# Moving accumulations between VectorE and ScalarE, filling PSUM banks earlier, and loading the first left-over tiles from SBUF

## The chip, the cores and the metric

The kernel runs on one core of a Trainium2 chip. The metric is the device time of one execution in microseconds (us). A core has a matrix engine (TensorE, PE in the profile), a vector engine (VectorE, DVE), an engine for activation functions that also copies and casts (ScalarE, ACT), a general one (GpSimd, POOL), and SyncE (SP), which here only issues DMAs. Each engine works through its own queue of instructions in order and waits on semaphores for what other engines have to finish first. PE reads from the on-chip memory SBUF and writes to PSUM, from which VectorE and ScalarE take the results. DMAs are issued from SP's queue and from ScalarE's queue (SPq and ACTq in the profile), and an issue stands in its engine's queue like any other instruction.

## The reference

One transformer block over a sequence of 2048 tokens with 576 features, in fp32. From a condition vector come six modulation vectors; then an attention with a memory carried over four segments of 512 tokens, and a gated MLP with 4608 hidden features:

```python
h = _layernorm(x) * (1 + ca) + sa
x = x + ga * _A_ref(h, A_wq, A_wk, A_wv, A_wo, A_beta)
h = _layernorm(x) * (1 + cb) + sb
g = _silu(h @ w_gate)
u = h @ w_up
x = x + gb * ((g * u) @ w_down)
```

The change touches the MLP and the passage from the attention to it, nothing inside the attention.

## The kernel before

**Precision.** Every fp32 operand of a matmul is split in two: a rounded part (`...h`, a cast on ScalarE) and the rest (`...l`, a subtraction on VectorE). A product takes three matmuls: high by high, high by low, low by high. So each operand costs one ScalarE and one VectorE instruction before PE can use it.

**Seven products for eight.** The MLP works on two halves of the tokens (t = 0 and 1, 1024 each) and, in each, on 18 blocks p of 256 hidden features. Inside a block the matrices are cut 2 by 2 and multiplied in seven products with sums and differences of the quarters (Winograd's form of Strassen's method). The operands for the tokens, seven sums m = 1 to 7 of them, lie in the tile `y`. The weights' sums are built by `sum_o` (L1410) in the tile `O`, and `prep_w` (L1413) splits them into `wh` and `wl`.

**A round.** One block p takes 14 steps k (loop at L1797): seven for the gate (z = 0) and seven for the up projection (z = 1). `step` (L1486) issues seven matmuls through `prod` (L1446): three for each of two pieces of 128 features, and one for the left-over 32 features, which are stored three times over (rows 0 to 31, 32 to 63 and 64 to 95: high, low, high) in the tiles `R[0]` and `R[1]` (`wr` in the profile). Results gather in the PSUM banks A, B and C, from which ScalarE copies (`copy_t`, L1480, and L1499) and VectorE adds (`fin`, L1462). The result of a round is the hidden block `AC`.

**Down projection.** The hidden block of round p is multiplied by `w_down` during round p + 1, between its steps. In `plain` rounds (t = 0, p = 0 to 6, and the last two blocks of both halves) eight groups of 12 matmuls do it. In the other rounds (t = 0, p = 7 to 15; t = 1, p = 0 to 15) it is done with seven products too: 14 groups c = 0 to 13 of six matmuls each (`down`, L1565), spread over the steps by `CH` (L37): one group a step, two in steps 4 and 11, none in steps 6 and 13. Group c belongs to product `POS[c // 2]`. Each product has an accumulator `acc` in SBUF that runs over all rounds.

**Banks and accumulators.** The results of a group go to a PSUM tile `pd` of tag `dn`, of which there are two, so group c + 2 uses that of group c. Most groups start a new sum in the bank, and VectorE adds it to the accumulator afterwards (L1584). The groups listed in `PA7` (L54), for t = 0, do otherwise: ScalarE first copies the accumulator into the bank (L1563), the matmuls add onto it, and ScalarE copies it back (L1580). The tile is claimed, and the accumulator put into it, at the top of the step in which the group runs (L1808 to L1810, `down_new`). In p = 7 the products 1, 5, 6 and 7 start anew, without an accumulator.

**Order.** The order of all this is written out by hand in the loop: what is issued in a step is in the order of the lines L1799 to L1917, for each engine. Subtractions on VectorE that belong to casts (`later`) run at the top of the next step, before the next products.

**Preparing the second half's operands.** While rounds p = 1 to 6 of t = 0 run, a generator `prep2` (L1264) builds the token operands of t = 1: twice per step, in steps 1 to 13, one turn is taken from it (L1915 to L1917). First five rows of 128 tokens are normalised: statistics on VectorE, two small instructions on GpSimd, the scaling on ScalarE (L1307), a store to DRAM (L1308), and the load of the row after next (L1289). Then for each of six pieces the columns are loaded back, transposed by PE into a `dn` bank (L1337), scaled, and the seven operands are formed, split and stored (`opr`, L1269).

**The first left-over tiles.** Before the first round, during the last projection of the attention (a loop over n = 0 to 31, L1721), the sums of the first left-over rows are built in a tile `RB` and split into `RH` (high, on ScalarE) and `RB` (low, on VectorE). `store_rb` (L1401) writes them three times to DRAM (`rD`) from ScalarE's queue at n = 12. `prep_r` (L1381) reads them back into `R[0]` and `R[1]` with six loads in SP's queue at n = 17 and 18. Later rounds read their left-over tiles from the same place in DRAM. At n = 24 ScalarE's queue issues the store of some weight sums (`store_o`). The loads of the first token operands `y` stand in SP's queue ahead of `prep_r`, and the stores of the projection's rows (`xD`, L883) among and behind it.

Of the kernel before, what the change touches and what calls it, by code (L numbers as in the profile page):

```python
# [15 lines left out]
P = 128  # L16
# [6 lines left out]
L = 512  # L23
# [29 lines left out]
P7 = 7  # L53
PA7 = (1, 3, 7, 9, 13)  # L54
WC = 4
# [46 lines left out]
def f32(ap):  # L102
    return ap.bitcast(F32)
# [3 lines left out]
def block(ctx: ExitStack, tc: tile.TileContext, x, wqk, wv, wo, beta, wgu, wrm, wd, c, w_mod, wm01, out):  # L107
# [1156 lines left out]
    def prep2(x2p):  # L1264
# [29 lines left out]
        for j, (sn, i) in enumerate(rows):  # L1294
# [10 lines left out]
            nc.gpsimd.tensor_scalar(nb, mv[:, 0:1], rs[:, 0:1], -1.0, op0=ALU.mult, op1=ALU.mult)  # L1305
            yield
            nc.scalar.activation(xl, xl, AF.Identity, scale=rs[:, 0:1], bias=nb[:, 0:1])  # L1307
            nc.sync.dma_start(xhD[sn][:, i, :], xl)  # L1308
            yield
            if j < 3:  # L1310
                load_row(j + 2)
            for _ in range(3):
                yield
        xbs = (xb, xl2[:, :L].rearrange("p (a b) -> p a b", b=P))
# [16 lines left out]
        for kb in range(3):  # L1331
            n = P if kb < 2 else 96
            for hv in range(2):
                for kh in range(2):
# [8 lines left out]
                    if j < 12:  # L1343
                        load(j)
                h00, h10, h01, h11 = [ha[:n, k, 256 * b:256 * b + 256] for k in range(2) for b in range(2)]
                nc.gpsimd.tensor_tensor(t3[:n], h11, h10, op=ALU.subtract)
                yield from opr(kb, hv, 0, h00)
                nc.gpsimd.tensor_tensor(h10, h10, h00, op=ALU.subtract)
                yield from opr(kb, hv, 5, t3[:n])
                yield from opr(kb, hv, 2, h11)  # L1350
                yield from opr(kb, hv, 3, h10)
                nc.gpsimd.tensor_tensor(h11, h11, h10, op=ALU.subtract)
                yield from opr(kb, hv, 1, h01)
                yield from opr(kb, hv, 4, h11)
                nc.gpsimd.tensor_tensor(h01, h01, h11, op=ALU.subtract)
                yield
                yield from opr(kb, hv, 6, h01)
# [37 lines left out]
    def split_rb(j):  # L1395
        r = RB[j]
        rh = RB[j, 1] = opl.tile([P, 7, P], F32R, tag="RH", name="RH")
        nc.scalar.copy(rh, r)
        later.append(lambda: nc.vector.tensor_tensor(r.bitcast(F32R), r, f32(rh), op=ALU.subtract))

    def store_rb(j):  # L1401
# [158 lines left out]
    def down_new(t, p, c):  # L1560
        pd = PD[c] = ps.tile([P, 2, L], F32, tag="dn", name="pd", bufs=2)
        if t == 0 and c in PA7 and (p > P7 or POS[c // 2] in (2, 3, 4)):
            nc.scalar.copy(pd[:, :, :288], down_acc(t, c))  # L1563

    def down(t, p, c):  # L1565
        m, q = POS[c // 2], c % 2
        ah, al = AP[p % 2, m]
        dh, dl = DP[p % 2, m]
        pd = PD.pop(c)
        new = p == (0 if t else P7) and m not in (2, 3, 4)  # L1570
# [8 lines left out]
        if on_act:  # L1579
            nc.scalar.copy(o, pd[:, :, :288])  # L1580
        elif new:
            nc.vector.tensor_copy(o, pd[:, :, :288])
        else:
            nc.vector.tensor_tensor(o, o, pd[:, :, :288], op=ALU.add)  # L1584

    def plain(t, p, c):
# [54 lines left out]
    with tc.manual_schedule():  # L1641
# [79 lines left out]
        for i in range(4):  # L1721
            for h in range(2):
                for c in range(WC):
# [16 lines left out]
                    elif n == 10:  # L1740
                        split_rb(0)
                    elif n == 12:
                        store_rb(0)
                    elif n in (17, 18):
                        prep_r(0, 0, n - 17)
                    if n == 24:
# [31 lines left out]
        for t in range(2):  # L1778
            for p in range(NPR):
# [17 lines left out]
                for k in range(14):  # L1797
# [8 lines left out]
                    while acts:  # L1806
                        acts.pop(0)()
                    if prev is not None and not is_plain(*prev):  # L1808
                        for j in range(CH[k]):
                            down_new(*prev, chunk + j)  # L1810
                    if dl and k in HP:
# [176 lines left out]
```

## Time and profile before

| | |
|---|---|
| median of three runs | 1814.87 us (1814.16 to 1815.64) |
| the profiled execution | 1814.78 us |
| its span, from the first to the last instruction | 1813.1 us |
| PE busy | 1765.0 us, 97% of the span |
| VectorE busy | 1495.2 us, 82% |
| ScalarE busy | 994.7 us, 55% |
| GpSimd busy | 485.3 us, 27% |

From 832 to 1152 us the rounds run whose down projections use `PA7`, nine in all; there PE is busy for 306.52 of 320 us, VectorE for 291.09, ScalarE for 199.08 and GpSimd for 135.13. The MLP begins near 543 us.

How to read the rows: times are in us, those of one instruction in groups in ns. A row of instructions in order of time has its start, its duration, engine, line, operation and tiles (output <- input), and in square brackets the idle time of the engine before it and what ended that (its releaser). A row of waits has the waiting instruction, what it waited for, the sum in us, how many times, and the longest. A group's row has the count, the busy time and the mean in ns, and behind the second bar the idle time just before. A window's row has its bounds and length, the busy time of PE, PE's weight loads, VectorE, ScalarE and GpSimd with the number of instructions, then the granted clock of PE, the DMA engines' busy share and GB/s. PE's matmuls overlap: a matmul on 512 columns is listed with 390 ns and the next starts 227 ns after it.

### The profile page before, as it was taken

To read this page: it belongs to the slowest core of one execution; us is meant where nothing else is said; L and a number is where in the kernel's file an instruction comes from. 1 tells how busy PE (TensorE), PEld (TensorE's weight loads), DVE (VectorE), ACT (ScalarE), POOL (GpSimd) and SP (SyncE) were. 2 spreads that over 40 slices of the span, in tenths; PEclk is the share of its full clock that TensorE was granted. 3 is DMA by queue.
4 is the path that set the end of the run, shared out by engine and by line. 5 is a ranking of instruction groups with operands and counts; after the bars stand their busy time and mean duration, and the time that the engine had idled before them with its cause. 6 is when DMAs were issued, how large, how long until landed. Compare 5 with 4: busy or idle time off the path is not lost.

```text
span 1813.1 us, 31431 instructions
## 1 busy us (share of the span) xinstructions
PE 1765.0 (97%) x10945; PEld 1494.4 (82%) x10945; DVE 1495.2 (82%) x3326; ACT 994.7 (55%) x2151; POOL 485.3 (27%) x748
## 2 busy tenths in 40 slices
PE   8999999999997999999999999999999999999999
PEld 5888867767776888888887888888888888888888
DVE  7567489999975787878999998868888888888886
ACT  6344578778864454544665666534544544544542
POOL 2100146555670654453354443100000000000000
PEclk9999999999998999999999999999999999999999
DMA  8678765577668677654443444495334324324331
GB/s 296 225 241 279 234 206 172 170 194 216 185 234 281 207 241 223 209 157 126 174 136 129 156 161 148 139 314 150 100 103 124 105 87 130 107 80 130 107 103 53
DMA packets 149190, 309.85 MB, mean 171 GB/s; under 512 B 28184, under 2 KB 60376, under 8 KB 147240
## 3 DMA queue, kind: packets, MB, share of 16 engines
q1 hardware_dynamic: 134824, 253.98, 45.8%
q10 hardware_dynamic: 14208, 53.86, 7.6%
q8 instruction: 87, 1.43, 0.3%
q14 instruction: 71, 0.58, 0.1%
HBM read 193.73 MB, written 113.33 MB: 169 GB/s over the span
## 4 chain that ended last, share of the span: by engine, by line
PE 73%; DVE 6%; DMA 3%; ACT 2%; issue 1%; POOL 1%; ACTq 0%; SPq 0%; DVEq 0%; POOLq 0%
PE A L1453 22%; PE pd L1576 14%; PE C L1453 11%; PE pd L1598 7%; PE B L1453 6%; PE av L768 3%; PE pw L876 2%; PE s L713 2%; PE s L742 2%; DVE wl L1418 1%; DVE sg L1529 1%; PE pn L1012 1%; DMA rD<-RB 1%; DVE acc L1584 1%; DMA wr<-rD 1%
## 5 line engine op out<-in xcount | busy, mean ns | idle before, releaser
L1453 PE MATMUL A<-y,wh 128*128 128x512 f32 x1152 | 404.2, 391 | 2.2 <-ACT B L1499 1.5
L1584 DVE TENSOR_TENSOR acc<-acc,pd 128x576 f32<-128x576 f32 x292 | 218.3, 750 | 66.2 <-PE pd L1576 59.6
L1418 DVE TENSOR_TENSOR wl<-O,wh 128x256 fp32r<-128x256 f32 x504 | 245.5, 492 | 11.3 <-ACT wh L1417 10.8
L1453 PEld LDWEIGHTS A<-y,wh 128*128 128x128 f32 x1152 | 216.5, 188 | 42.5 <-ACT tb L1482 1.9
L213 DVE CUSTOM_DVE_ANT_0 junk<-s,tri 128x384 bf16<-128x384 f32 (+3 forms) x512 | 218.4, 486 | 22.7 <-PE s L742 8.7
L1453 PE MATMUL A<-y,wl 128*128 128x512 f32 x576 | 224.7, 390 | 0.0
L1576 PE MATMUL pd<-dh,ah 128*128 128x288 f32 x700 | 209.4, 299 | 13.5 <-ACT pd L1563 8.6
L1576 PE MATMUL pd<-dl,ah 128*128 128x288 f32 x700 | 206.1, 294 | 0.0
L1576 PE MATMUL pd<-dh,al 128*128 128x288 f32 x700 | 205.1, 293 | 0.0
L1453 PE MATMUL C<-y,wh 128*128 128x512 f32 x576 | 202.5, 392 | 0.0
L1417 ACT CAST wh<-O 128x256 fp32r<-128x256 f32 x504 | 199.4, 405 | 4.8 <-issue 2.9
L1523 DVE TENSOR_TENSOR al<-sg,ah 128x512 fp32r<-128x512 f32 x219 | 160.7, 734 | 10.9 <-ACT ah L1522 10.7
L1522 ACT CAST ah<-sg 128x512 fp32r<-128x512 f32 x219 | 136.0, 621 | 54.0 <-DVE sg L1477 38.9
L1576 PEld LDWEIGHTS pd<-dh,ah 128*128 128x128 f32 x700 | 131.4, 188 | 31.6 <-ACT pd L1563 12.0
L1408 POOL TENSOR_TENSOR O<-O 128x256 f32<-128x256 f32 x132 | 114.1, 882 | 137.6 <-DMA O<-in_wgu_dram 66.2
L749 ACT ACTIVATE Pt<-s 128x512 f32<-128x512 f32 x256 | 135.4, 598 | 22.3 <-PE s L742 13.2
L1576 PEld LDWEIGHTS pd<-dl,ah 128*128 128x128 f32 x700 | 132.4, 189 | 12.3
L1576 PEld LDWEIGHTS pd<-dh,al 128*128 128x128 f32 x700 | 132.1, 189 | 0.0
L1453 PE MATMUL A<-y,wr 128*128 128x512 f32 x288 | 113.9, 395 | 10.4 <-DMA wr<-rD 10.4
L1453 PEld LDWEIGHTS C<-y,wh 128*128 128x128 f32 x576 | 108.0, 188 | 18.9
L1453 PEld LDWEIGHTS A<-y,wl 128*128 128x128 f32 x576 | 108.3, 188 | 15.4
L1469 ACT ACTIVATE sg<-sg 128x512 f32<-128x512 f32 x73 | 46.2, 633 | 124.5 <-DVE sg L1468 124.5
(422 smaller groups left out, 4320.0 us busy)
## 6 DMA issues: line engine op xcount, KB each, us to landing
wr<-rD SPq DMA_DIRECT2D x213, 112.0 KB
O<-in_wgu_dram SPq DMA_DIRECT2D x36, 512.0 KB
O<-oD SPq DMA_DIRECT2D x36, 512.0 KB
oD<-O ACTq DMA_DIRECT2D x34, 512.0 KB
ks<-kD SPq DMA_DIRECT2D x64, 216.0 KB
qs<-qD SPq DMA_DIRECT2D x64, 216.0 KB
O<-in_wgu_dram SPq DMA_DIRECT2D x36, 384.0 KB
y<-yD SPq DMA_DIRECT2D x11, 1024.0 KB
```

Of the source, the lines that this page charges most:

```text
L213: nc.vector.tensor_tensor_reduce(junk[:, :n], bank[:, o:o + n], tri[:, L - n:], 1.0, -3e38, op0=ALU.add, op1=ALU.max, accum_out=mcol[u][0] ...
L749: nc.scalar.activation(pt[:, h], bank, AF.Exp, scale=SCALE)
L768: nc.tensor.matmul(av[u][32 * h:32 * h + 32, 128 * j:L], lhsT=vq[s][:, j, VW * hh:VW * hh + 32], rhs=pt[:, h, c:c + L - 128 * j], start=(j ...
L1408: eng.tensor_tensor(o[:, d], o[:, a], o[:, b], op=op)
L1417: nc.scalar.copy(wh, o)
L1418: later.append(lambda: nc.vector.tensor_tensor(wl, o, f32(wh), op=ALU.subtract))
L1453: nc.tensor.matmul(bank, lhsT=a, rhs=b, start=(first and n == 0), stop=(n == 6), skip_group_check=not first)
L1522: nc.scalar.copy(ah, src)
L1523: later.append(lambda: nc.vector.tensor_tensor(al, src, f32(ah), op=ALU.subtract))
L1576: nc.tensor.matmul(pd[:, i, :288], lhsT=a[:, tk], rhs=w, start=(first and k == 0), stop=(k == 2), skip_group_check=not first)
L1584: nc.vector.tensor_tensor(o, o, pd[:, :, :288], op=ALU.add)
L1598: nc.tensor.matmul(pd[:, i, :288], lhsT=a[:, tk], rhs=w, start=(k == 0), stop=(k == 5))
```

## The change

There are three parts. (1) `PA7` names nine groups in place of five, and groups 7, 9 and 13 leave it. A `pd` tile is no longer claimed at the top of the step: `down` claims those of its own and the next group if that has not been done (t = 1: its own alone), and at its end, for t = 0, that of group c + 2, or of the first groups of the next round; ScalarE's copy of the accumulator into the bank is issued there, right behind the emptying of the same bank. (2) In `prep2` a row's scaling stands four turns behind its statistics, with its store and the load of the row after next directly behind it; one turn is added between the two transposes of a piece and one is taken out before the last operand; the subtractions stand earlier, and the operands come in the order 0, 2, 1, 5, 3, 4, 6. The number of turns stays the same. (3) `first_r` at n = 12 copies the first left-over tiles with six DMAs in ScalarE's queue from `RH` and `RB` straight into `R[0]` and `R[1]`; the loads at n = 17 and 18 are gone, and the store to DRAM stands at n = 28.

```diff
-PA7 = (1, 3, 7, 9, 13)
+PA7 = (0, 1, 2, 3, 4, 6, 8, 10, 12)
...
-            yield
+            for _ in range(4):
+                yield
             nc.scalar.activation(xl, xl, AF.Identity, scale=rs[:, 0:1], bias=nb[:, 0:1])
             nc.sync.dma_start(xhD[sn][:, i, :], xl)
-            yield
             if j < 3:
                 load_row(j + 2)
-            for _ in range(3):
-                yield
+            yield
...
+                    if kh == 0:
+                        yield
                 h00, h10, h01, h11 = [ha[:n, k, 256 * b:256 * b + 256] for k in range(2) for b in range(2)]
                 nc.gpsimd.tensor_tensor(t3[:n], h11, h10, op=ALU.subtract)
+                nc.gpsimd.tensor_tensor(h10, h10, h00, op=ALU.subtract)
                 yield from opr(kb, hv, 0, h00)
-                nc.gpsimd.tensor_tensor(h10, h10, h00, op=ALU.subtract)
-                yield from opr(kb, hv, 5, t3[:n])
                 yield from opr(kb, hv, 2, h11)
-                yield from opr(kb, hv, 3, h10)
                 nc.gpsimd.tensor_tensor(h11, h11, h10, op=ALU.subtract)
                 yield from opr(kb, hv, 1, h01)
+                nc.gpsimd.tensor_tensor(h01, h01, h11, op=ALU.subtract)
+                yield from opr(kb, hv, 5, t3[:n])
+                yield from opr(kb, hv, 3, h10)
                 yield from opr(kb, hv, 4, h11)
-                nc.gpsimd.tensor_tensor(h01, h01, h11, op=ALU.subtract)
-                yield
                 yield from opr(kb, hv, 6, h01)
...
+    def first_r():
+        for z in range(2):
+            for c in range(3):
+                v = RB[0] if c == 1 else f32(RB[0, 1])
+                nc.scalar.dma_start(f32(R[z][32 * c:32 * c + 32]), v[32 * z:32 * z + 32])
...
     def down_new(t, p, c):
-        pd = PD[c] = ps.tile([P, 2, L], F32, tag="dn", name="pd", bufs=2)
+        pd = PD[t, p, c] = ps.tile([P, 2, L], F32, tag="dn", name="pd", bufs=2)
         if t == 0 and c in PA7 and (p > P7 or POS[c // 2] in (2, 3, 4)):
             nc.scalar.copy(pd[:, :, :288], down_acc(t, c))
 
+    def ahead(t, p, c):
+        v = (p + c // 14, c % 14)
+        if (t, *v) not in PD and not is_plain(t, v[0]):
+            down_new(t, *v)
+
     def down(t, p, c):
+        for j in range(c, c + 2 - t):
+            ahead(t, p, j)
...
-        pd = PD.pop(c)
+        pd = PD[t, p, c]
...
+        if t == 0:
+            ahead(t, p, c + 2)
...
                     elif n == 12:
+                        first_r()
+                    elif n == 28:
                         store_rb(0)
-                    elif n in (17, 18):
-                        prep_r(0, 0, n - 17)
...
-                    if prev is not None and not is_plain(*prev):
-                        for j in range(CH[k]):
-                            down_new(*prev, chunk + j)
```

## The prediction

> **What bounds the kernel now.** I read the page's head first, then the list of what TensorE (PE) waited for, because PE is busy almost throughout.
>
> ```profile
> span 1813.1 us, 31431 instructions
> PE 1765.0 (97%) x10945; PEld 1494.4 (82%) x10945; DVE 1495.2 (82%) x3326; ACT 994.7 (55%) x2151; POOL 485.3 (27%) x748
> ...
> PE A L1453 <- DMA wr<-rD: 10.4, 1, 10.4
> PE pd L1576 <- ACT pd L1563: 8.6, 8, 1.8
> ...
> PE pd L1576 <- DVE acc L1584: 4.9, 7, 1.1
> ...
> PE A L1453 <- ACT B L1499: 1.5, 1, 1.5
> ...
> PE pt L1337 <- DVE acc L1608: 0.8, 2, 0.4
> PE A L1453 <- ACT tb L1482: 0.7, 1, 0.7
> ```
>
> PE has 48 us of idle time in the span (1813.1 - 1765.0), and no edit here takes a matmul away, so those 48 us and slowed matmuls are all there is to win. The waits quoted add up to 26.9 us, and each of the three edits points at some of them: the second and third line at the accumulators, the first at the left-over tiles, the last three at the operand preparation. Next, two windows: one in the first half of the MLP, while sums are accumulated in seven products, and one in the second half.
>
> ```profile
> 900.00:1000.00 100.00, 95.73 (x510) 82.20 (x509) 93.51 (x141) 62.88 (x137) 42.02 (x42) 1.00 0.44 145
> ...
> 1300.00:1400.00 100.00, 100.00 (x545) 88.09 (x544) 86.77 (x163) 48.66 (x113) 0.00 (x0) 1.00 0.34 105
> ```
>
> The columns are PE, PEld, DVE, ACT and POOL busy time. In the first half VectorE (DVE) is at 94% and PE has gaps; in the second DVE is at 87%, GpSimd (POOL) is idle, and PE has none. The same matmuls run in both, so the second half gives the floor. I take it from the chain of waits, from the second step of a round (bank C) to that of a later round.
>
> ```profile
> 889.79 1.62 PE C L1453 x7
> ...
> 1137.91 1.62 PE C L1453 x7
> ...
> 1160.27 1.60 PE pd L1598 x12
> ...
> 1224.91 1.59 PE C L1453 x7
> ...
> 1292.03 1.59 PE C L1453 x7
> ```
>
> The first two rows are seven rounds apart: 248.12 / 7 = **35.45 us** a round. The last two are two rounds apart: 67.12 / 2 = **33.56 us**. (The row between is a group of another stage, for edit 3.) Nine rounds (t = 0, sums of p = 7 to 15) thus lose up to 9 x 1.89 = 17.0 us, of which the waits show 13.5 and slower starts after them the rest.
>
> **Edit 1: accumulators.** One round in order of time shows both waits.
>
> ```profile
> 881.86 1.41 DVE L1584 TENSOR_TENSOR acc<-acc,pd 128x576 f32<-128x576 f32 x2
> ...
> 881.97 0.62 ACT L1522 CAST ah<-sg 128x512 fp32r<-128x512 f32 x1 [1.56 <-DVE sg L1529]
> ...
> 882.66 0.40 PE L1576 MATMUL pd<-dh,ah 128*128 128x288 f32 x1 [0.83 <-DVE acc L1584]
> ...
> 885.84 0.63 ACT L1469 ACTIVATE sg<-sg 128x512 f32<-128x512 f32 x1 [2.94 <-DVE sg L1468]
> ...
> 888.05 0.64 ACT L1563 COPY pd<-acc 128x576 f32<-128x576 f32 x1
> ...
> 888.74 0.40 PE L1576 MATMUL pd<-dh,ah 128*128 128x288 f32 x1 [1.82 <-ACT pd L1563]
> ```
>
> At 882.66 group 6 waits for its bank: DVE, late in its queue, empties groups 4 and 5 only then. At 888.74 group 7 waits for ScalarE (ACT) to put its accumulator into the bank; that copy stands in ACT's queue behind a Silu that waited 2.94 us for DVE, and behind DMA issues and casts. After the change groups 0 to 4, 6, 8, 10 and 12 are ACT's, so 0, 2, 4, 6, 8, 10 and 12 leave DVE, and 7, 9 and 13 come to it; group 7 needs no copy at all, and group 6 gets its copy behind the emptying of group 4, in the same bank. So the 1.8 us wait loses its cause, and the 0.8 us one comes to hang on ACT in place of DVE. The prices:
>
> ```profile
> L1418 DVE TENSOR_TENSOR wl<-O,wh 128x256 fp32r<-128x256 f32 x118 | 68.6, 592 | 0.0
> ...
> L1584 DVE TENSOR_TENSOR acc<-acc,pd 128x576 f32<-128x576 f32 x72 | 53.2, 748 | 9.8 <-PE pd L1576 8.5
> ...
> L1580 ACT COPY acc<-pd 128x576 f32<-128x576 f32 x42 | 26.9, 642 | 28.5 <-PE pd L1576 28.5
> ...
> L1563 ACT COPY pd<-acc 128x576 f32<-128x576 f32 x40 | 25.7, 642 | 0.0
> ```
>
> (groups by line of 845 to 1145 us). DVE loses 4 x 0.748 = 3.0 us a round: from 0.9351 x 35.45 = 33.1 to 30.1. ACT gains 4 emptyings and 4 fillings, 8 x 0.642 = 5.1 us: from 0.6288 x 35.45 = 22.3 to 27.4, which is 81% of a round of 33.8. Both fit under PE. What is late next: in every second round ACT casts a left-over tile in the step of groups 4 and 5, just ahead of emptying group 4, so group 6 may still wait a few tenths there; and group 1's new filling sits behind DVE's emptying of group 13, with ACT's casts of the next operands queued behind it, which are used a round later. I leave 0.3 us a round for all this, an estimate a little under half of the 0.83 us wait: 9 x (35.45 - 33.86) = **14.3 us** gained. Bounds: 17.0 above; below, what rivals A (6.3) and C (0) give.
>
> Against this stands a rule of the Trainium skill ("SBUF — State Buffer", section "Who interferes with whom"): a VectorE instruction with two SBUF inputs contends with a GpSimd instruction that reads SBUF, and one with at most one SBUF input, as the accumulation from PSUM is, does not. The trace agrees as far as it goes: wl, with two SBUF inputs, takes 592 ns here and 492 over the whole run (row under rival A). By that rule the change takes away the very instructions that never met GpSimd; the sum by it is rival A's.
>
> In the second half the bank is now claimed just ahead of its use and not one step ahead; claiming issues nothing, and PE has no gap to lose or win there: 0, covered by the full PE of the 1300 window.
>
> **Edit 2: first left-over tiles.** Today they go SBUF to DRAM and back:
>
> ```profile
> 535.06 0.81 ACTq L1404 DMA_DIRECT2D rD<-RH  x2
> ...
> 536.18 14.41 DMA rD<-RB
> 550.66 0.32 SPq L1384
> ...
> 551.49 3.73 DMA wr<-rD
> ...
> 555.36 0.77 PE L1453 MATMUL A<-y,wr 128*128 128x512 f32 x1 [10.45 <-DMA wr<-rD]
> ...
> 559.34 0.53 PE L1453 MATMUL A<-y,wl 128*128 128x512 f32 x1
> ```
>
> The store takes 14.41 us, the load 3.73, and PE stands for 10.45. Then it runs slowly: nine matmuls in 555.36 to 559.34, 0.44 us apart, against 1.59 / 7 = 0.227 in the chain rows: 3.98 - 2.04 = 1.9 us more. Ceiling 12.4 us. After the change six 112 KB copies go from SBUF straight into the tiles, half the bytes of the store. Bounds on their landing: 3.73 us after 535.06, or 14.41 us after 536.18, when 550.6 would leave 5.7 us of the wait. Half the bytes of the slow row, 7.2 us, puts them at 543.4, ahead of PE's need (555.36 - 10.45 = 544.9). I take this: no wait for them.
>
> What stands behind the new issues:
>
> ```profile
> SPq L1361 <- DMA rD<-RH: 7.7, 1, 7.7
> ...
> L1384 ACTq DMA_DIRECT2D wr<-rD x3: 328/378/432, 1193.8 to 1194.7; - x3
> ...
> 536.86 0.58 ACT L855 CAST hh<-pto 128x512 fp32r<-128x512 f32 x1
> ...
> 539.61 0.37 PE L876 MATMUL pw<-woh,hh 128*128 128x288 f32 x1 [0.58 <-DVE xr L881]
> ...
> 547.22 0.32 SPq L1361 DMA_DIRECT2D y<-yD  x1
> ...
> ACT cu L1482 <- PE A L1453: 10.1, 1, 10.1
> ```
>
> Three more issues on ACT's queue are 3 x 0.378 = 1.1 us; the cast hh behind them ends at 537.44, PE needs it at 539.61, so 2.2 us cover that. But the first row shows that an issue can wait for an earlier DMA that it has nothing to do with (a load on SP's queue, 7.7 us for a store from ACT's). If ACT's last copies wait so for the first to land, at some 541, hh ends near 542 and PE is 2.5 us late. I take 1.5 of these. The six loads leave SP's queue, so the y load at 547.22 and what follows it come no later. The store to DRAM now stands, with three issues, ahead of the copy cu, for which PE's third step waits; today ACT idles 10.1 us there. For this I take 0.5. Together 12.4 - 2.0 = **10.4 us**; bounds 12.4 and, with rival B, 4.
>
> **Edit 3: operand preparation.** The same instructions in other places: a row's scaling stands four turns behind its statistics and not one, the next row's load directly behind a store, and subtractions earlier.
>
> ```profile
> ACT ha L1307 <- POOL nb L1305: 8.0, 3, 4.2
> ACT xl L1307 <- POOL nb L1305: 7.5, 2, 3.9
> ```
>
> Up to 4.2 us ACT stands before a scaling, and what is queued behind it, the copies B and tb, is what PE waits for in the 1.5 and 0.7 us rows. Three turns more are one and a half steps, each of 7 matmuls for products and, mostly, 12 for sums, 3.2 us (1.6 each in the chain rows): 4.8 us, more than the 4.2. With the 0.8 us of transposes that wait for DVE the ceiling is 3.0 us; new is that the first load of the next part follows the last row's store by one turn and not four, and holds SP's queue until that store has landed. I put that at 1 us, an estimate from the two 0.4 us waits that PE has at these transposes today: 3.0 - 1.0 = **2.0 us**, bounds -1.0 (the new wait alone) and 3.0.
>
> **The sum** is made against the profiled execution's 1814.78 us, of which 1.7 lie around the span, unchanged, and which stands 0.09 us under the median of 1814.87: 1814.78 - 14.3 - 10.4 - 2.0 = **1788.1 us**.
>
> **Rivals.**
>
> A: DVE stays the bound of the nine rounds. For it: 94% busy, and its instructions are longer where POOL works beside it.
>
> ```profile
> L1418 DVE TENSOR_TENSOR wl<-O,wh 128x256 fp32r<-128x256 f32 x504 | 245.5, 492 | 11.3 <-ACT wh L1417 10.8
> ```
>
> If the denser rest collides so much more that half of the 3.0 us is eaten, DVE has 31.6 us of work a round. On a line between the two windows (86.8%: nothing lost; 93.5%: 1.89 us lost) this settles at a round of about 34.75 (90.9%, 1.2 lost): 9 x 0.7 = 6.3 us gained, **1796.1 us**. Against it: the freed instructions lie in the steps where PE waits, since groups 0, 2, 4 and 6 leave DVE there, and 7, 9 and 13 come back only later in the round.
>
> B: the left-over tiles land as late as the store does, 14.41 us after their issue. Of the 12.4 us the wait's rest of 5.7 and the slow restart of 1.9 stay, with the 0.5 of above: 4.3 gained, **1794.2 us**. For it: the loads that filled the DMA engines then are still there. Against it: half the bytes, and no second trip.
>
> C: the wait only changes its name. The bank of group c + 2 is that of group c, so a filling can't start before the bank is emptied; if ACT empties group 4 as late as DVE did, group 6 waits for ACT, and the nine rounds gain nothing: **1802.4 us**. Against it: in the round shown ACT idles for the 1.56 us up to 881.97, just where emptying and filling (1.28 us) would go.
>
> D, on the other side: ACT becomes the bound of the nine rounds. Its emptyings wait for PE, 28.5 us in 42, 0.68 each (the L1580 row), in order, with everything behind them. Four more cost 2.7 us a round, and the copies 5.1: 7.8. Today 35.45 - 22.3 = 13.2 us of ACT's round are idle; if they can't take this in, because each of them waits for a fixed point of PE or DVE, the round grows to 43.2 and the kernel by 9 x 7.8 = 70 less 12.4: **1872 us**. It decides from where more than 9.4 us of idle time stay in a round: 27.4 + 9.4 = 36.8, that is 12.4 / 9 above today's 35.45. Against it: in the second half such waits shrink as PE runs on without gaps.
>
> **How the numbers follow.** The forecast has 0.57, A 0.17, B 0.12, C 0.06, D 0.05; 0.03 are for several small losses that cancel the gain. The predicted time is the forecast's, 1788. All ceilings together, 17.0 + 12.4 + 3.0 = 32.4, give 1782.4 as the lower end; A and B together (6.3 + 4.3 + 2.0 = 12.6) give 1802.2, and C 1802.4, so the upper end is 1803. Beyond it lie D, the cancelling losses and a part of C. Faster means by more than 0.2%, 3.6 us, about what a measurement of this kernel can tell from no change: forecast, A, B and C, 0.92; within it 0.03; slower D, 0.05.
>
> **What would show it.** Edit 1: rounds 33.6 to 34.1 us apart in the chain, PE's waits for accumulators under 3 us in all, ACT near 81% and DVE near 89% in the 900 window. Rounds of 34.7 with DVE above 90% are A; waits of some 0.8 us for ACT at group 6 are C; ACT above 90% is D. Edit 2: no wait of PE for a left-over tile near 545 us; a short one for the cast hh near 540 us shows ACT held by its DMA issues; a wait of 5 us or more is B. Edit 3: the scaling no longer waits for POOL, and the waits for B and tb are gone. The forecast is wrong if the rounds stay at 35 us or more, or if the 10.4 us wait comes back as one for the y loads or for a later left-over tile.

## The result and the profile after

The changed kernel takes 1803.77 us (median, 1803.12 to 1806.46) where the kernel before, on the same chip, takes 1815.26. The ratio of the runs is 0.9933 [0.991, 0.9956], with its 95% interval in brackets; that is 12.2 us less (the two medians are 11.5 us apart). The forecast was 1788.1 with 1782.4 to 1803.0 around it: the direction was right, less than half of the gain came, and the time lies just above the range. The head of the page of the changed kernel and its list of PE's waits (the profiled execution took 1806.46 us):

```profile
span 1804.7 us, 31494 instructions
PE 1762.7 (98%) x10945; PEld 1496.8 (83%) x10945; DVE 1473.2 (82%) x3290; ACT 1032.2 (57%) x2221; POOL 486.2 (27%) x748
...
PE pw L876 <- DVE xr L881: 9.9, 3, 8.8
PE pd L1589 <- ACT acc L1593: 8.8, 8, 1.4
...
PE A L1459 <- ACT tb L1488: 2.0, 1, 2.0
```

Work moved as planned: VectorE is busy 22 us less than before, ScalarE 37.5 us more. Of the waits before, the 10.4 us for the left-over tile, 8.6 us for ScalarE's filling and 4.9 us for VectorE's emptying are gone. But 8.8 us stand in the attention's last projection, 8.8 us at the accumulators, and 2.0 us at the copy tb. Each edit has its own successor wait. The window from 900 us, and then from the chain of waits the same step in four rounds:

```profile
900.00:1000.00 100.00, 97.02 (x525) 84.79 (x524) 86.42 (x130) 77.72 (x166) 48.23 (x49) 1.00 0.46 142
```

```profile
832.00 1.62 PE C L1459 x7
...
877.67 1.63 PE C L1459 x7
...
1087.46 1.62 PE C L1459 x7
...
1144.55 1.59 PE C L1459 x7
```

VectorE's share has fallen from 93.5% to 86.4% and ScalarE's has risen from 62.9% to 77.7%, so neither is the bound, and PE still has gaps. In the chain the first and the last of these rows are nine rounds apart, 312.55 us, where nine rounds at the 35.45 us of before are 319.05: **6.5 us** gained. From 877.67 to 1087.46, six rounds, a round takes 34.97 us, against the forecast's 33.86.

**Where PE waits at the accumulators.** One place in order of time:

```profile
875.06 0.95 ACT L1398 CAST RH<-RB 128x896 fp32r<-128x896 f32 x1
...
875.90 0.66 ACT L1593 COPY acc<-pd 128x576 f32<-128x576 f32 x1
876.43 0.67 ACT L1569 COPY pd<-acc 128x576 f32<-128x576 f32 x1
...
876.61 0.40 PE L1589 MATMUL pd<-dh,ah 128*128 128x288 f32 x1 [1.41 <-ACT acc L1593]
...
899.46 0.64 ACT L1569 COPY pd<-acc 128x576 f32<-128x576 f32 x1 [2.50 <-DVE acc L1597]
```

At 876.61 group 5, one of VectorE's, waits for the emptying of group 4, which ends at 875.90 + 0.66 = 876.56. The filling that starts at 876.43, group 6's, begins before that emptying ends, so it belongs to the other bank, and group 5 is in the bank of group 4 and not in that of group 3. In the program as built, the two `dn` banks (called a and b here) go to the groups of a round like this, in seven of the nine rounds (p = 8 to 14; the first and the last differ a little):

```
group           0 1 2 3 4 5 6 7 8 9 10 11 12 13
changed kernel  a b a b a a b b a a b  b  a  a
```

(in the next round with a and b exchanged). `ps.tile` is called in the order of the groups, but a bank is given where a tile is first used. A ScalarE group is first used by its early filling, a VectorE group only by its own matmuls. So group 6 takes the bank that group 3 left, and group 5 gets what comes free next, the bank of group 4, whose emptying is the latest thing before it. Groups 7, 9, 11 and 13 stand in the bank of the group just ahead of them as well. The row at 899.46 is another wait that the prediction had named: the filling for group 1 of the next round stands 2.50 us behind VectorE's emptying of group 13. PE has no gap there.

**Where PE waits for the left-over tiles' copies.** The rows of ScalarE, VectorE and PE around them in order of time, a wait of SyncE's queue, a row of the chain, then the windows:

```profile
535.23 0.52 ACTq L1405 DMA_DIRECT2D wr<-RB  x1
...
538.36 0.52 ACTq L1405 DMA_DIRECT2D wr<-RB  x1
543.26 0.51 ACTq L1405 DMA_DIRECT2D wr<-RH  x1
543.82 0.40 ACT L1423 CAST wh<-O 128x256 fp32r<-128x256 f32 x1 [9.44 <-DMA wr<-RH]
544.13 0.58 ACT L855 CAST hh<-pto 128x512 fp32r<-128x512 f32 x1
...
544.74 0.69 DVE L859 TENSOR_TENSOR hl<-pto,hh 128x512 fp32r<-128x512 f32 x1 [8.84 <-ACT hh L855]
...
546.28 0.45 DVE L881 TENSOR_TENSOR xr<-pw,xr 128x288 f32<-128x288 f32 x1
...
546.88 0.58 PE L876 MATMUL pw<-woh,hh 128*128 128x288 f32 x1 [8.80 <-DVE xr L881]
```

```profile
SPq L1361 <- DMA wr<-RH: 7.3, 1, 7.3
```

```profile
546.88 5.48 PE pw L876 x28
```

```profile
530.00:540.00 10.00, 6.95 (x50) 6.28 (x48) 5.20 (x9) 1.25 (x2) 7.57 (x13) 1.00 1.04 332
540.00:550.00 10.00, 3.12 (x13) 3.15 (x14) 4.74 (x10) 4.84 (x10) 0.00 (x0) 0.50 0.95 281
```

ScalarE's last two issues stand at 538.36 and 543.26. The trace also records when each DMA signals its landing, with 16 events. By these the issue at 538.36 begins once a load of y has landed, at 538.34, and the one at 543.26 once the copy issued at 535.23 has landed, at 543.24, 8.0 us after its issue; the later DMA signals on the same semaphore as the earlier one. SyncE's queue was held in the same way: the issue of a load of y waited 7.3 us for the first copy. The casts stand right behind the last issue. (The profile names another copy at the cast wh, by the time of an event at 543.78; the copy that was issued at 536.43 lands at 545.82, when the cast has long run, so it isn't the cause.) Then come hh, VectorE's hl, a few VectorE instructions, and the sum xr, which frees the bank that PE wants. PE could have gone on at 546.88 - 8.80 = 538.08. The DMA engines are busy throughout (shares of 1.04 and 0.95) with loads of y of 1 MB among others, and the first four copies of 112 KB took 7.4 to 9.4 us from issue to landing.

**Where PE waits for tb.** VectorE, ScalarE and PE in the third round:

```profile
606.55 0.34 SPq L1289 DMA_DIRECT2D ha<-xD  x1
...
612.95 0.82 DVE L1300 BATCH_NORM_STATS2 st<-ha 128x6 f32<-128x288 f32 x2 [2.18 <-DMA ha<-xD]
...
616.13 0.68 DVE L1482 TENSOR_TENSOR cu<-C,tb 128x512 f32<-128x512 f32 x1
616.93 0.59 ACT L1488 COPY tb<-A 128x512 f32<-128x512 f32 x1 [3.73 <-DVE cu L1482]
...
617.57 0.50 PE L1459 MATMUL A<-y,wh 128*128 128x512 f32 x1 [2.01 <-ACT tb L1488]
```

VectorE's statistics stand in front of a row that has not landed. Behind them in its queue is the sum cu, which reads the old tb; ScalarE may write the new one only after it, and PE's bank is freed by that copy. Counted from a round's first matmul to the next one's, this third round takes 40.4 us, against 37.5 before.

### The profile page after: what moved, and what is told of

Read it like the earlier page. It is cut to its first block, busy times and chain, and to the rows that moved or that the text cites. A ratio compares the mean times of both kernels' runs of the same rounds, so it can differ in the third digit from the quotient of the medians.

```text
span 1804.7 us, 31494 instructions
## 1 busy us (share of the span) xinstructions
PE 1762.7 (98%) x10945; PEld 1496.8 (83%) x10945; DVE 1473.2 (82%) x3290; ACT 1032.2 (57%) x2221; POOL 486.2 (27%) x748
## 4 chain that ended last, share of the span: by engine, by line
PE 72%; DMA 4%; DVE 4%; ACT 4%; issue 1%; POOL 1%; ACTq 0%; SPq 0%; DVEq 0%; POOLq 0%
PE A L1459 22%; PE pd L1589 14%; PE C L1459 11%; PE pd L1613 6%; PE B L1459 6%; PE pw L876 3%; PE av L768 3%; PE s L713 2%; PE s L742 2%; PE pn L1012 1%; DVE junk L213 1%; ACT acc L1593 1%; DMA O<-in_wgu_dram 1%; DMA y<-yD 1%; DMA wd<-dr__15586 1%
## 5 line engine op out<-in xcount | busy, mean ns | idle before, releaser
L1597 DVE TENSOR_TENSOR acc<-acc,pd 128x576 f32<-128x576 f32 x258 | 193.7, 751 | 64.6 <-PE pd L1589 58.9
L1459 PE MATMUL C<-y,wl 128*128 128x512 f32 x288 | 112.2, 389 | 0.0
```

The source lines that it names most:

```text
L1459: nc.tensor.matmul(bank, lhsT=a, rhs=b, start=(first and n == 0), stop=(n == 6), skip_group_check=not first)
```

## The experiments

The theories are numbered anew in each group of runs. Part 2 of the change is the prediction's edit 3, part 3 its edit 2. Each ratio is against the kernel before, run beside it. Where a time is given for one stage, it is counted from the start of a matmul to that of a later one in the profiled executions: "the passage" is from the 200th matmul ahead of the MLP's first to the first of its second round, "the nine rounds" are those whose down projections use `PA7`. Before, these take 61.7 and 319.0 us, in the changed kernel 58.5 and 312.6.

### The three edits one by one

The kernel before with one part of the diff each. Part 1 (e1_acc):

```diff
-PA7 = (1, 3, 7, 9, 13)
+PA7 = (0, 1, 2, 3, 4, 6, 8, 10, 12)
...
+        if t == 0:
+            ahead(t, p, c + 2)
```

Part 3 (e2_tiles):

```diff
                     elif n == 12:
+                        first_r()
+                    elif n == 28:
                         store_rb(0)
-                    elif n in (17, 18):
-                        prep_r(0, 0, n - 17)
```

Part 2 (e3_prep):

```diff
-            yield
+            for _ in range(4):
+                yield
             nc.scalar.activation(xl, xl, AF.Identity, scale=rs[:, 0:1], bias=nb[:, 0:1])
```

> The kernel before with edit 1 alone (nine groups by ScalarE, banks claimed and filled ahead). Theory 1, from the trace of the changed kernel: its rounds are 34.92 us apart where they were 35.45, so nine rounds gain 4.8 us, about 1810 us; group 5 waits 0.8 to 1.4 us a round for ScalarE to empty group 4. Rival (the edits only work together, the rounds are slowed by what edit 3 or 2 leaves behind): rounds near 33.9 us and some 1801 us for edit 1 alone.

> The kernel before with edit 2 alone (left-over tiles copied in ScalarE's queue). Theory 2: ScalarE is held at its fifth and sixth DMA issue until earlier DMAs have landed, some 9 us, and TensorE stands 8.8 us in the attention's last projection in place of 10.4 us in the MLP's first step: a gain of 2 to 4 us, 1811 to 1813 us, no wait for a left-over tile, but one of 8 to 9 us for VectorE's sums near 538 us. Rival (that wait is a chance of one execution or comes from edit 3): a gain of 8 to 12 us, 1803 to 1807 us.

> The kernel before with edit 3 alone (order of the operand preparation). Theory 3, from the changed kernel's list of waits (2.0 for tb, 0.2 for B and 0.3 for the transposes where there were 0.7, 1.5 and 0.8): 0.5 us gained, 1814 to 1816 us, no change that can be told. The prediction: 2.0 us gained, near 1813 us, with no wait for B and tb.

Measured: part 1 alone 1806.89 us, 0.9944 [0.9922, 0.9966]; part 3 alone 1815.69, 0.9992 [0.998, 1.0004]; part 2 alone 1814.30, 0.9988 [0.9977, 1.0]. Of 1815.85 that is 10.2, 1.5 and 2.2 us, together 13.9 against the change's 12.2: they add up within their intervals. PE's waits in the three, one kernel after the other:

```profile
PE pd L1583 <- ACT acc L1587: 8.8, 8, 1.4
```

```profile
PE pw L876 <- DVE xr L881: 10.1, 3, 9.0
PE pd L1582 <- ACT pd L1569: 8.6, 8, 1.8
```

```profile
PE A L1453 <- ACT tb L1482: 1.8, 1, 1.8
```

Each successor wait comes with its own edit: the 8.8 us at the accumulators with part 1, the 9.0 us in the projection with part 3 (in place of the load's 10.4), the tb of 1.8 us with part 2. So the three waits do not need one another.

Part 1's nine rounds take 312.5 us, as in the changed kernel: 6.5 us gained, where theory 1 had 4.8 and the rival, which expected rounds near 33.9, falls. What its time gained beyond that lies outside these rounds and is not explained by the edit. Part 3 alone can't be told from no change by its time, where 2 to 4 us had been expected. In its profiled execution the passage is 2.6 us shorter than before, but the nine rounds take 3.0 us more: PE's granted clock fell there twice, behind waits of 1.8 us that the kernel before has too, without a fall (see the last section).

### Banks under two names

The changed kernel, with the groups' tiles given to two tags by the parity of c, so that a bank follows from the group's number:

```diff
-        pd = PD[t, p, c] = ps.tile([P, 2, L], F32, tag="dn", name="pd", bufs=2)
+        pd = PD[t, p, c] = ps.tile([P, 2, L], F32, tag=f"dn{c % 2}", name="pd", bufs=1)
```

(the plain rounds' tiles and the transposes' take the two tags in turn).

> The changed kernel with the two banks under two names, groups with even c in one and with odd c in the other (the other users of the banks take them in turn as before), so that group 5 gets group 3's bank and not group 4's. Theory 1 (group 5 waits because a bank is given in the order of first use, and the early filling for group 6 takes the bank that group 3 left): the waits for ScalarE's emptying, 8.8 us, go, rounds come to 33.6 to 34.1 us, 1794 to 1797 us. Rival A (VectorE is the bound): rounds stay above 34.6 us, 1801 us or more. Rival C (ScalarE empties group 4 too late in any case): group 6 waits in place of group 5, by as much, 1802 to 1804 us.

Measured: 1792.77 us (1791.42 to 1796.0), 0.9868 [0.9847, 0.9888]. The banks now go a b a b through all 14 groups. No wait for a bank of `pd` in these rounds is left in the list, and the chain has (the two inner rows are for the next section)

```profile
832.57 1.62 PE C L1465 x7
842.94 1.61 PE C L1465 x7
...
1078.26 1.61 PE C L1465 x7
...
1134.32 1.59 PE C L1465 x7
```

nine rounds in 301.75 us: 17.3 us less than before, where the prediction had 17.0 us as this edit's ceiling. The theory that the bank's order costs the rest (theory 1) holds: with nothing but the naming of the banks different, 10.8 us of nine rounds (312.55 - 301.75) come back. Rounds and time came out a little better than the 33.6 to 34.1 and the 1794 to 1797 us expected, and no wait moved to group 6, so rivals A and C fall.

### The nine groups or the placing

The next question is what of those 17 us the move from VectorE to ScalarE brings, and what the early placing. This kernel is e7_pool (below; 1790.03 us, rounds as in e4_banks) with the old five groups.

```diff
-PA7 = (0, 1, 2, 3, 4, 6, 8, 10, 12)
+PA7 = (1, 3, 7, 9, 13)
```

> The run with 1790.0 us with the five groups of the kernel before for ScalarE (1, 3, 7, 9, 13) instead of nine: it tells what of the first edit is the accumulators' early placing with a bank of their own, and what the move of work from VectorE. Theory 1a (both are needed): VectorE's 291 us of work in the nine rounds were 91% of 319.6 us and would be 96% of 302.4 us, so it becomes the bound in places: rounds of 33.9 to 34.8 us against 33.6, VectorE's accumulations waited for again, 1793 to 1800. Theory 1b (the placing alone brings it all, the move costs and gives nothing): rounds of 33.6, 1789 to 1791.

Measured: 1797.73 us, 0.9899 [0.9883, 0.9914], against 0.9851 [0.9817, 0.9885] for e7_pool: apart by 0.5%, with intervals that just touch. Its list of waits, its chain and its window:

```profile
PE pd L1594 <- DVE acc L1602: 7.8, 8, 1.2
```

```profile
852.98 1.61 PE C L1464 x7
...
1096.63 1.61 PE C L1464 x7
```

```profile
1000.00:1100.00 100.00, 97.23 (x526) 84.71 (x525) 94.47 (x141) 64.53 (x138) 46.00 (x47) 1.00 0.47 156
```

Seven rounds in 243.65 us are 34.81 each, against 35.45 before and, over the same seven rounds of e4_banks, (1078.26 - 842.94) / 7 = 33.62. Counted over all nine rounds, which take 319.0, 311.4 and 301.8 us, the placing with banks of its own gains 7.6 us with the five groups, and the move of work then another 9.6. VectorE is at 94% and PE waits for it again. Theory 1a holds: both halves are needed. The move is the larger part in this order; the move without the placing was not run.

### Who holds the projection

Three other ways to fill the first left-over tiles, and one kernel that leaves them empty. e5_sp is the changed kernel with the copies in SP's queue; the other three are e4_banks with one edit. In e5_sp:

```diff
-                nc.scalar.dma_start(f32(R[z][32 * c:32 * c + 32]), v[32 * z:32 * z + 32])
+                nc.sync.dma_start(f32(R[z][32 * c:32 * c + 32]), v[32 * z:32 * z + 32])
```

In e6_early the same, and at n = 12 (the two loads stood before the loop):

```diff
-                        first_r()
+                        first_r(0)
+                        load_y(0, 5)
+                        first_r(1)
+                        load_y(0, 3)
```

In e7_pool, with z = 0 ahead of the clears of `y` and z = 1 behind them:

```diff
-                nc.scalar.dma_start(f32(R[z][32 * c:32 * c + 32]), v[32 * z:32 * z + 32])
+            nc.gpsimd.tensor_copy(R[z][32 * c:32 * c + 32], v[32 * z:32 * z + 32])
```

In e8_none, which clears the tiles and so leaves out the first round's left-over products:

```diff
-                nc.scalar.dma_start(f32(R[z][32 * c:32 * c + 32]), v[32 * z:32 * z + 32])
+            nc.gpsimd.memset(f32(R[z][0:96]), 0.0)
```

> The changed kernel with one edit: the six copies that fill the first left-over tiles are issued on SP's queue instead of ScalarE's, at the same point of the program. Theory 1 (ScalarE is held by issuing these copies until about 543.8 us, so the cast hh, VectorE's hl and the sum xr come late and TensorE stands 8.8 us in the attention's last projection): that wait is gone, ScalarE's idle stretch of 9.4 us before the cast wh is gone too. In SP's queue the copies stand behind the last loads of y, which are issued at about 542.8, so they land about 546 to 547 and TensorE waits 1.5 to 3 us for them at the first left-over product: 1803.8 - 8.8 + 2.3 = about 1797. Theory 2 (the projection is late for another cause, for instance the transfers' traffic or VectorE's own queue, and ScalarE's issues only happen to lie beside it): the wait in the projection stays at 8 us or more and the time stays at 1802 to 1805.

> The changed kernel with the accumulators' banks under two names (as in the run with 1792.8 us) and the copies on SP's queue, three of them ahead of the two last loads of y, three between these. Theory 1 (held ScalarE): 1792.8 - 8.8 = 1784 if the first tile's copies land by about 544.7, and up to 3 us more if they come late or push the loads of y back: 1784 to 1787. Theory 2 (the projection is late anyway): 1791 to 1794.

> The changed kernel with the banks under two names, and the first left-over tiles filled by six GpSimd copies of 32x896 in place of six transfers, three ahead of the seven clears of y and three behind them; no transfer is issued for them at all. The clears of the same size took 0.8 us each, an addition of GpSimd 2.5 ns an element, so a copy takes 0.8 to 2.3 us, and the first tile is whole by 537 to 541.5 us. Theory 1: no wait in the projection and none for the left-over tile: about 1784 (1783 to 1786). Theory 2: 1791 to 1794. If the clears of y now come late for the first products (they would end by 540 to 545, needed from about 544.7), 1 us more.

> The changed kernel with the banks under two names, and the first left-over tiles cleared by GpSimd instead of filled: the copies are left out, so the first round's left-over products count as zero. It gives the most that the second edit could bring. Theory 1: the wait of 8.8 us is gone and none for a tile is left: 1784 (1783 to 1785.5), 12 us or so being what the forecast had as the edit's ceiling against the kernel before. Theory 2: 1791 to 1794, since the projection would be late without the copies too.

Measured: e5_sp 1805.11 us, 0.9934 [0.9908, 0.9959]; e6_early 1792.43, 0.9866 [0.9841, 0.9891]; e7_pool 1790.03, 0.9851 [0.9817, 0.9885]; e8_none 1789.17, 0.9846 [0.9818, 0.9874]. First e5_sp, its waits and two rows of its chain:

```profile
PE A L1459 <- DMA wr<-RH: 8.6, 1, 8.6
```

```profile
528.60 16.94 DMA y<-yD
...
547.29 4.67 DMA wr<-RH
```

Once ScalarE no longer issues the copies, 0.9 us of waits are left in the projection, so theory 1 (ScalarE held) is right and theory 2 falls, although the time of 1805 us is the one that theory 2 had. The gain didn't come: SP's queue itself was held until a load of y landed, 16.94 us after its start, the first tile's copies were issued only at 546 to 547 us (the expectation had 542.8), and PE stood 8.6 us for them. Then e6_early, e7_pool and e8_none, PE's waits there:

```profile
PE C L1464 <- DMA y<-yD: 6.5, 1, 6.5
...
PE A L1464 <- DMA wr<-RH: 1.2, 1, 1.2
```

```profile
PE pw L876 <- DVE xr L881: 2.5, 3, 1.0
...
PE A L1464 <- DMA y<-yD: 0.5, 1, 0.5
```

```profile
PE C L1463 <- DMA y<-yD: 2.9, 1, 2.9
```

With the copies put ahead, PE waits 1.2 us for them and 6.5 us for the load of y that they pushed back, 7.7 in all: the miss of 6 us or so against the expected 1784 to 1787. (By its time alone e6_early would have gone to theory 2; the projection's waits, 1.1 us, speak against it.) So as transfers the copies cost PE about 8 us of waits in each of the three places tried. Without them (e8_none) 2.9 us for y are left. Filled by GpSimd, which had time there, nothing over 1 us is left at this place:

```profile
537.58 1.02 POOL L1410 CAST wr<-RB 32x896 fp32r<-32x896 f32 x1
```

What that is worth shows in the passage. With the copies as transfers it takes 59.1 us in e2_tiles, 58.3 in e4_banks, 59.5 in e5_sp and 58.2 in e6_early; with GpSimd's copies 49.7 in e7_pool and 50 to 52 in the three kernels built on it. That is 6 to 10 us less, one profiled execution each. In the whole time it is blurred: the medians of e4_banks and e7_pool are only 2.7 us apart, their intervals overlap, and e6_early, e7_pool and e8_none came out 5 to 8 us above the expected 1784. One reason is in e7_pool's profiled execution: its second and third rounds take 3.4 us more than those of e4_banks, with a fall of the granted clock in the third. Why y is late by 2.9 us in e8_none and by 0.5 in e7_pool stays open.

### What makes tb late

Two kernels on e7_pool's ground. The first puts a row's scaling three turns behind its statistics and leaves two behind it; the second takes back that half of part 2 altogether and keeps the new order of the operands.

In e9_three:

```diff
-            for _ in range(4):
+            for _ in range(3):
                 yield
...
-            yield
+            for _ in range(2):
+                yield
```

In e10_order:

```diff
-            for _ in range(4):
-                yield
+            yield
             nc.scalar.activation(xl, xl, AF.Identity, scale=rs[:, 0:1], bias=nb[:, 0:1])
             nc.sync.dma_start(xhD[sn][:, i, :], xl)
+            yield
             if j < 3:
                 load_row(j + 2)
-            yield
+            for _ in range(3):
+                yield
```

> The run with 1790.0 us (banks under two names, GpSimd's copies) with one edit: a row's scaling stands three turns behind its statistics instead of four, and two turns are left behind it instead of one, so that from the load of a row to its statistics there are seven turns instead of six (eight in the kernel before). Theory 3 (TensorE's 2.0 us for the copy tb, and the third round's 40.3 us against 37.5 before, come from VectorE, whose queue is held by the statistics of a row that has not landed; the addition cu and with it ScalarE's copy tb stand behind them): VectorE's waits for the row's load shrink from 8.5 us in three to about the 3.6 us in one of the kernel before, the wait for tb to 1 us or less, the third round to 38 to 39 us; the time falls by 0.5 to 1.5 us, too little to tell from the time alone. Rival (tb is late from the new order of the operands): the wait stays at 1.8 us and the round at 40.

> The run with 1790.0 us with the first half of the third edit undone (scaling one turn behind the statistics, the next row's load two turns behind it, as before), the new order of the operands kept. Theory 3: the wait for tb falls to 0.8 us or less and the third round to 37.5 to 38.5 us, but the wait of 1.5 us for the copy into B that the kernel before had in the second round comes back (37.2 us instead of 35 to 36); the time stays within 1 us. Rival (the order of the operands makes tb late): tb stays at 1.8 us, the third round at 40 us, B comes back, 1 to 2 us slower.

Measured: e9_three **1785.15 us** (1782.1 to 1787.49), 0.9826 [0.9806, 0.9847]; e10_order 1788.53, 0.9844 [0.9826, 0.9863]. The intervals overlap with each other and with e7_pool's. The waits from 555 to 660 us decide, first in e9_three, then in e10_order; in the changed kernel the statistics wait for 8.5 us in three times, B for 0.2 and tb for 2.0:

```profile
DVE st L1306 <- DMA ha<-xD: 5.6, 2, 4.9
...
PE A L1465 <- ACT B L1511: 0.8, 1, 0.8
```

```profile
DVE st L1306 <- DMA ha<-xD: 3.7, 1, 3.7
...
PE A L1465 <- ACT B L1511: 1.7, 1, 1.7
...
PE A L1465 <- ACT tb L1494: 0.7, 1, 0.7
```

With seven turns from load to statistics tb is gone from the list and B costs 0.8; with eight, as before, tb is 0.7 and B 1.7, close to the 1.5 before. The third round takes 37.5 us in e9_three and 37.0 in e10_order, against 40.3 in e7_pool. The order of the operands is the same in all three, so the rival falls. It is not the sum of VectorE's waits that counts (e9_three still has 4.9 us in one), but the third of them, 2.2 us in the changed kernel and 2.0 in e7_pool just ahead of the late sum cu; it is gone in both new kernels. Four turns of delay fixed one wait and made another; three fix most of both. By its median e9_three is the fastest version here, 31 us or 1.7% below the kernel before, and 18.6 us below the changed kernel's. Its median is 4.9 us below e7_pool's, where 0.5 to 1.5 were expected; in the profiled executions 3.3 us lie in the six rounds that the operand preparation runs in, and part of them is the fall of the clock in e7_pool's third round.

## Why the prediction was wrong, step by step

**What bounds the kernel: right.** The three places named were the ones to win at. e9_three, which mends all three edits, gets 31.3 us; the prediction's three ceilings added up to 32.4. By stages of the profiled executions the changed kernel gains 6.5 us in the nine rounds (edit 1) and 3.2 in the passage (edit 2), and loses 1.0 in the six rounds of the operand preparation (edit 3), where 14.3, 10.4 and 2.0 us of gain were forecast.

**Edit 1: 14.3 us forecast, 6.5 in the rounds (alone, by its time, 10.2 with 6.2 to 14.2 around it).** The step that failed is that group 6 gets its copy "behind the emptying of group 4, in the same bank"; behind it stands the statement, in the kernel's description and in rival C, that the bank of group c + 2 is that of group c. It is so in the kernel before, where claiming and first use have one order. The change parts the two, and a bank goes by first use. The prediction looked for the remaining wait at group 6, with 0.3 us a round; it was at group 5, 1.41 us in rounds with the left-over cast (the row at 875.06, just ahead of the emptying) and 0.79 in the others, 1.1 on average (8.8 / 8). The round then fits: 33.86 - 0.3 + 1.1 = 34.7, against 34.7 (nine rounds) to 35.0 (six of them) measured; what the last 0.3 us are is not shown. The rest of the step was right: VectorE was freed, ScalarE had room (80% in e9_three's window from 900 us, with no gap of PE; forecast 81%), the ceiling was 17.3 us against 17.0. Rival A (VectorE stays the bound) is refuted for the change, although its rounds of 34.7 came: VectorE is at 86.4% there, and with mended banks and the same work on VectorE the rounds take 33.53 us. It describes e11_five instead. The rule of the Trainium skill ("SBUF — State Buffer", section "Who interferes with whom") that was set beside rival A did not decide: the accumulations taken off VectorE freed it whether or not they meet GpSimd, for 9.6 us of the nine rounds. Rival C came nearest in time, 1802.4 against 1803.8, but not by its mechanism alone: it let the rounds gain nothing and edits 2 and 3 their full 12.4 us. Rival D (ScalarE becomes the bound) is refuted by the same rounds, with ScalarE at 80%.

**Edit 2: 10.4 us forecast, 1.5 measured alone by its time, 3.2 in the passage of the changed kernel.** The mechanism, that an issue in ScalarE's queue can wait for an earlier DMA to land, was named, and the landing was sized well (7.2 us estimated; the first tile's three copies took 7.4, 8.0 and 8.6 us). The term taken from it was mis-sized: "PE is 2.5 us late", of which 1.5 were charged. Three things were missing. The hold ends at 543.8 and not at 541: the last issue waits not for the first copy, which lands at 541.50, but for the second. Behind hh stand hl and xr in VectorE's queue, so PE starts at 546.88 and not when hh ends. And PE's need had moved ahead, to 538.08 from 539.61. So PE stood 8.8 us in spite of the cover of 2.2 us. The 1.9 us of slow restart, counted as gained, were paid again: 28 matmuls in 5.48 us, where at full clock they start 0.13 us apart. Rival B did not come as such: no copy took 14.41 us, and PE did not wait for a left-over tile. But its ground, DMA engines that other loads fill, was the better reading of that stage: in the places tried, the cost of the transfers only moved (e5_sp, e6_early), and the passage got shorter without them (e7_pool).

**Edit 3: 2.0 us forecast, 2.2 [0, 4.2] measured alone, none in its rounds.** The two numbers agree by luck. The six rounds that the edit touches take 221.6 us in the changed kernel and 221.0 in e3_prep, against 220.6 before, so nothing was gained there. The wait for B fell from 1.5 to 0.2 us as forecast, but the one for tb, which was to vanish, grew from 0.7 to 2.0. The step says that "the next row's load" moves directly behind a store and looks for what that costs at the next part's first load; it didn't count the turns from a row's load to that row's statistics, eight before and six after, so VectorE came to wait for the row, and tb behind it.

## What to carry to other kernels

Where a buffer is given at first use, an early first use by one engine reorders the buffers for all others; tie the buffer to the index, or read the assignment from the built program. Before putting DMA issues in the queue of a computing engine, look at whether the DMA engines are full there: here an issue stood until an earlier DMA had landed, and everything behind it in that queue, and behind that in the next engine's queue, was the price. In this case a copy by an engine with time to spare beat all three ways of issuing the transfers. And compare stages as well as times: a gain of about 9 us in one stage was hardly to be seen in the medians.

## What the runs showed of the hardware

PE's granted clock can fall after a short pause. In the traces' record of it the clock is 1.00 or 0.50, and between the program's start and its end a fall lasts 3.41, 6.83 or 10.24 us; a window's figure is a mean. At the wait of 8.80 us it was 0.50 for 10.24 us, as in the window from 540 us. After the waits of 1.41 us it stayed at 1.00. But after the one of 2.01 us at 617.57 it fell too, for 3.41 us from 618.53; the changed kernel's window behind it:

```profile
620.00:625.00 5.00, 5.00 (x28) 4.70 (x27) 2.14 (x4) 2.11 (x6) 1.36 (x2) 0.81 0.96 250
```

The Trainium skill ("TensorE: Matmul & The Clock Gate", section "Part 1: The HAM clock gate") puts the fall at an idle window of about 3.4 us; the 8.80 us agree, and the pause of 2.01 us in this trace is shorter, so here the measurement decides.

The length of the pause alone does not decide it. In e8_none PE waited 2.04 us for tb, at 616.00, and the clock stayed:

```profile
615.00:620.00 5.00, 4.00 (x23) 3.58 (x24) 3.86 (x7) 3.95 (x9) 1.05 (x1) 1.00 0.41 110
```

The waits of 1.8 us at the accumulators brought two falls in e2_tiles and none before. So with such waits the time of a kernel can differ from one execution to the next, by an estimated 1.7 us for a fall of 3.41 us to half the clock.

The first four copies of 112 KB inside SBUF took 7.4 to 9.4 us in ScalarE's queue, with the DMA engines full. In e5_sp the first three took 4.7 to 5.3 us in SP's queue, at a DMA share of 0.97 from 545 to 550 us. GpSimd moved the same rows to other partitions in 1.02 us.
